# Copying a partial sum out of its PSUM bank, spreading GpSimd's weighings over three experts, and moving one addition ahead of a transposition

## The chip, the cores and the metric

The kernel runs on one core of a Trainium2 chip. The metric is the device time of one execution in microseconds; lower is better. Three timed runs of the kernel before gave 933.78, 928.51 and 932.78, so the median is 932.78 us. The execution that the profiler recorded took 928.73 us, of which 927.0 lie between its first and its last instruction.

## The reference

Two blocks follow each other. The first is an attention with polynomial sketches: 4 batches, 4 heads, 1088 positions, head dimension 32. Its output, laid out as 4352 tokens of 128 numbers, is the `x` of the second block, a mixture of experts that is balanced by Sinkhorn iterations:

```
logits = x @ w_gate                      # 4352 tokens, 8 experts
P = exp(logits - logits.max())
for _ in range(8):                       # rows, then columns, are normalised
    P /= P.sum(1, keepdims=True) + 1e-09
    P /= P.sum(0, keepdims=True) + 1e-09
    P *= N / E
for e in range(E):
    h = np.maximum(x @ w1[e], 0.0)       # 128 -> 1024
    ye = h @ w2[e]                       # 1024 -> 128
    out += P[:, e:e + 1] * ye
```

All is fp32. Every token passes through all eight experts, so nearly all the work is the two layers of the experts.

## The kernel before

**Groups and experts.** The tokens stand along the free axis of `xT` (128 features by 4352 tokens). The list `groups` cuts the expert work into (first token, columns of a tile, tiles, experts, weighted). The first eight groups are plain: expert 0 for all tokens and expert 1 for the first 1280 tokens are computed before the weights P are known, and their unweighted results are kept in SBUF, in `kept[0]` and `kept[1]`. These eight run while attention and Sinkhorn still go on; a hand-written generator (`steps`, fed by `fill`) deals out the expert work a step at a time between the parts of attention and routing. Then follow five weighted groups of three tiles of 256 tokens (first tokens 1280, 512, 2048, 2816, 3584) with experts 1 to 7 (2 to 7 for the group at 512), and a last one of two tiles of 256 tokens at token 0 with experts 2 to 7. For a weighted group GpSimd multiplies the group's columns of `xT` with the row of P (`weigh`, line 693, tile `xe`), since a positive factor passes through the relu. One expert of a three-tile group takes about 18.7 us.

**A step.** In each step TensorE does one first-layer product into one of four banks named `a` (line 929), ScalarE applies the relu and writes it to SBUF (line 933, tiles `hb` and `hx`), and TensorE does second-layer products of eight steps before (line 1114) into four banks named `s`. The second layer is multiplied with fewer products by Strassen-like schemes: seven products for two tiles (function `seven`), twenty for three. VectorE forms the sums of relu blocks that such schemes need (lines 946 and 993), GpSimd the sums of the second layer's weights (tiles `ws`, lines 203 to 206 and 242).

**Ends of plain groups.** In a plain group of two tiles that uses the seven products (five groups: three with 416 columns, two with 384), bank 0 ends up with P1 in its lower 64 partitions, and P1 and others go together into the two output tiles `y1` and `y2`, which are columns of `kept`. The function `part_of_seven(g, k)` is called when bank k has got its last product. ScalarE copies what has to change partitions or be read twice; VectorE adds. `add_now` queues an addition for the current step, `add` for a later step at leisure. For k = 0 ScalarE makes `z` from the two halves of the bank (lines 762 and 763), and VectorE adds the bank to it (line 756, `z<-s,z`). For k = 1 ScalarE copies bank 1 to `m` (line 768), and VectorE adds P1, still in bank 0, and `m` into the lower half of `y1` (line 756, `kept<-s,m`). The pool of the banks holds one buffer for each name, so the next group's first product into bank 0 waits for the last reader of bank 0.

**Weighing what was kept.** Once P is known, the kept results must be weighted too. `weigh_kept(g)` does this for a weighted group: for each expert that the group doesn't compute itself (one, or two for the groups at tokens 512 and 0), it loads the row of P, broadcast to 128 partitions, through SyncE's queue (tile `pb`, line 689) and lets GpSimd multiply (line 693, `kept<-kept,pb`); then GpSimd adds two kept results to one (line 717), and for the last group forms a difference (line 720). All of it is called at one place in `steps`: in the first step of the group's fourth expert (third in the last group). GpSimd's instructions are kept in program order.

**The end.** `last_part(g, k)` assembles the last group. Bank 3 comes first, then 0, 2, 1. For k = 2 VectorE does two additions into `y2`, then `put(y2)` transposes it in blocks of 32 and stores it by four DMAs (two on SyncE's queue, two on ScalarE's), then VectorE adds to the upper half of `x`. For k = 1 it adds bank 1 and `x` into `y1`, transposes and stores it. In this last stretch, from the second last block on, VectorE, TensorE and ScalarE run in the order in which the program writes them; for VectorE and TensorE that also holds while attention and routing run.

Of the kernel before, what the change touches and what calls it, by code (L numbers as in the profile page):

```python
# [50 lines left out]
def kernel(  # L51
# [12 lines left out]
    nc = tc.nc  # L64
# [50 lines left out]
    own = consts.tile([P, H], F32, name="own")  # L115
# [36 lines left out]
    for i in range(2):  # L152
        t = wk.tile([P, H + 1, NT + 1, D], F32, name=f"v{i}", bufs=1)
# [487 lines left out]
    lower, upper = slice(0, H2), slice(H2, P)  # L641
# [17 lines left out]
    kept = [keep.tile([P, N], F32, name="kept0"), keep.tile([P, 1280], F32, name="kept1")]  # L659
# [4 lines left out]
    def direct_of(j):  # L664
        return items[j][0] in DIRECT
# [21 lines left out]
    def weights_of(e, lo, n, tag):  # L687
        pb = pools[0].tile([P, 3 * NT3], F32, tag=tag, name=tag)[:, 0:n]
        tc.keep_in_program_order(nc.sync.dma_start(out=pb, in_=pT[e:e + 1, lo:lo + n].to_broadcast([P, n])))
        return pb  # L690

    def weigh(out, x, pb):
        tc.keep_in_program_order(nc.gpsimd.tensor_tensor(out, x, pb, op=Alu.mult))  # L693
# [12 lines left out]

    first_weighted = next(j for j, (g, e) in enumerate(items) if g == PLAIN)

    def weigh_kept(g):

        lo, n, t, es, _ = groups[g]
        ys = []
        for e in range(es[0]):
            ys.append(kept[e][:, lo:lo + n * t])
            weigh(ys[e], ys[e], weights_of(e, lo, n * t, "pb"))
        for y in ys[1:]:
            tc.keep_in_program_order(nc.gpsimd.tensor_tensor(ys[0], ys[0], y, op=Alu.add))
        if t == 2:
            k1, k2 = ys[0][upper, 0:n], ys[0][upper, n:2 * n]
            tc.keep_in_program_order(nc.gpsimd.tensor_tensor(k1, k1, k2, op=Alu.subtract))  # L720

    def at_leisure(do):

        soon.append(lambda: later.append(do))

    def put(y, lo, n, queues):
        b0, nb = lo // 32, n // 32
        yt = pools[0].tile([P, NT3 // 32, 32], F32, tag="yt", name="yt", bufs=4)[:, 0:nb, :]
        nc.vector.transpose(out=yt.rearrange("p b d -> p (b d)"), in_=y)
        store(yt, b0, b0 + nb, queues)  # L730
# [13 lines left out]
    def room(tag, n=NMAX):  # L744
        return keep.tile([P, NMAX], F32, tag=tag, name=tag)[:, 0:n]

    def part_of_seven(g, k):

        lo, n, _, es, _ = groups[g]
        s = sums[g][k]  # L750

        def add(out, a, b):
            at_leisure(lambda: nc.vector.tensor_tensor(out, a, b, op=Alu.add))

        def add_now(out, a, b):
            soon.append(lambda: nc.vector.tensor_tensor(out, a, b, op=Alu.add))  # L756

        own = parts.setdefault(g, {})
        y1, y2 = (kept[es[0]][:, lo + t * n:lo + (t + 1) * n] for t in range(2))
        if k == 0:  # L760
            z = own["z"] = room("z", n)
            nc.scalar.copy(z[lower], s[upper])
            nc.scalar.copy(z[upper], s[lower])
            add_now(z, s, z)
            own["p1"] = s
        elif k == 1:
            m = own["m"] = room("m", n)
            nc.scalar.copy(m, s)
            add_now(y1[lower], own["p1"][lower], m[lower])
        elif k == 2:  # L770
            w, f = own["w"], own["f"] = room("w", n), room("f", n)
            nc.scalar.copy(w[lower], s[lower])
            nc.scalar.copy(f[lower], s[upper])
            nc.scalar.copy(f[upper], s[upper])
        else:
            r = room("r", n)
            nc.scalar.copy(r[upper], s[lower])
            own["r"] = r
            own["p7"] = s
        own[k] = True  # L780
        z, w, f, m = (own.get(x) for x in "zwfm")
        if all(own.get(x) for x in (0, 2, 3)) and "v" not in own:
            own["v"] = True
            add_now(w[upper], own["p7"][upper], own["r"][upper])
            add(z, z, w)
            add(y2, z, f)
        if all(own.get(x) for x in range(4)):
            add(y1[upper], z[upper], m[upper])
# [9 lines left out]
    def last_part(g, k):  # L798


        lo, n, *_ = groups[g]
        s0, s1, s2, s3 = sums[g]

        def add(out, a, b):
            nc.vector.tensor_tensor(out, a, b, op=Alu.add)

        (y1, y2), z, w, x, f, r = last_rooms(g)
        if k == 3:
            nc.scalar.copy(r[upper], s3[lower])
            add(w[upper], s3[upper], r[upper])  # L810
        elif k == 0:
            nc.scalar.copy(z[upper], s0[lower])
            nc.scalar.copy(f, s0)
            add(x[upper], z[upper], w[upper])
            add(z[upper], x[upper], s0[upper])
        elif k == 2:
            nc.scalar.copy(r[lower], s2[upper])
            nc.scalar.copy(x[lower], s0[lower])
            add(y2[upper], z[upper], s2[upper])
            add(y2[lower], s2[lower], r[lower])  # L820
            put(y2, lo + n, n, (nc.sync, nc.scalar))
            add(x[upper], x[upper], s2[upper])
        else:
            add(y1, s1, x)
            put(y1, lo, n, (nc.sync, nc.scalar))
# [295 lines left out]
    def second(k, p):  # L1121
        into(items[blocks[k][0]][0], *p)

    def steps():

        todo, sums_at, t = {}, {}, 0
        for k in range(len(blocks) + 5):
            if k == len(blocks) - 2:
                ctx.enter_context(tc.manual_schedule(engines={engines.DVE, engines.PE, engines.Activation}))
            if k == len(blocks):  # L1130
                for i, ps in enumerate(last_products()):
                    todo.setdefault(t + i, []).extend(ps)
            if k < len(blocks):
                j, q = blocks[k]
                g, e = items[j]
                lo, n, tiles, es, weighted = groups[g]
                if q == 0:
                    for i in (j, j + 1, j + 2 if 0 < j and j + 2 < first_weighted else j):
                        if i < len(items) and i not in sources and (pools or i < first_weighted):
                            prepare_x(i)  # L1140
                        if i < len(items) and i not in loaded_w and (pools or i < first_weighted):
                            prepare_w(i)
                if j == 0 and q == 2:
                    prepare_w(2)
                if q == 1 and j + 1 < first_weighted and not direct_of(j + 1) and loaded_w[j + 1][2] is None:
                    w1, w2, _ = loaded_w[j + 1]
                    w = w1, w2, sums_of_two(items[j + 1][1], w2)
                    loaded_w.update({i: w for i in loaded_w if items[i][1] == items[j + 1][1]})
                if q == 0:
                    if weighted and e == es[3 if tiles == 3 else 2]:  # L1150
                        weigh_kept(g)
                if k == len(blocks) - HELD:
                    kept_to_sums(g)
                m, step, sums_ = (four if tiles == 3 else two)(k)
                products = twenty if tiles == 3 else eight if g in DIRECT else seven
            for c in range(m if k < len(blocks) else 4):
                if k < len(blocks):
                    step(c)
                for do in sums_at.pop(t, ()):
                    do()  # L1160
                while soon:
                    soon.pop(0)()
                for b, p in todo.pop(t, ()):
                    second(b, p)
                if k < len(blocks) and c == 0:
                    for i in range(2, 10):
                        sums_at.setdefault(t + i, []).append(lambda i=i, f=sums_: f(i))
                    if k < len(blocks) - 2:
                        for i, ps in enumerate(products(k)):
                            todo.setdefault(t + LAG + i, []).extend((k, p) for p in ps)  # L1170
                share = n / 480 * (16 / 15 if g in DIRECT else 1)
                if k >= len(blocks):
                    while later:
                        later.pop(0)()
                elif later and (tiles == 3 or c % 2 or share > 0.9):
                    later.pop(0)()
                yield share
                t += 1
        while soon:
            soon.pop(0)()  # L1180
        while later:
            later.pop(0)()
# [105 lines left out]
```

## Time and profile before

| What | Value |
|---|---|
| time, median of three | 932.78 us |
| span of the profiled execution | 927.0 us |
| VectorE busy from 110 to 215 us | 90.09 of 105 us |
| ScalarE busy from 110 to 215 us | 57.18 of 105 us |
| GpSimd busy over the span | 211.3 us (23%) |
| last instruction of VectorE that computes | ends at 923.48 us |

The profile's engines are PE (TensorE's matmuls), PEld (its weight loads), DVE (VectorE), ACT (ScalarE), POOL (GpSimd) and SP (SyncE, which issues most DMAs). A row of a timeline gives the start in us from the first instruction, the duration, the engine, the source line, the operation, what is written and read by the program's names, the shape, how many instructions were merged into the row, and in brackets how long the engine stood idle before it and what released it. TensorE executes each fp32 matmul of the program as two records, and two halves of 64 columns run side by side, so that a row "x4" is one step of one layer.

By stages, attention lies mostly in the first 110 us, the five ends of plain groups lie at about 118, 141, 163, 182 and 203 us, Sinkhorn's iterations run beside them on VectorE until about 175 us, and weighted groups fill the time from 203 us to the end.

### The profile page before, as it was taken

What the parts mean: (1) busy time and instruction counts of PE and PEld (TensorE: products, weight loads), DVE (VectorE), ACT (ScalarE), POOL (GpSimd) and SP (SyncE); (2) the same over time, 40 slices, a digit from 0 to 9 for tenths busy, and PEclk for the clock granted to TensorE, in tenths of its full rate; (3) what the DMA queues carried; (4) which work ended last, traced back from release to release, by engine and by line L of the source; (5) the groups of instructions that cost most, each with busy time, mean ns of one, the idle gap of its engine ahead of it and who ended that gap; (6) DMA issues with size and microseconds to landing.
All of it is one profiled execution on the core that took longest, in us unless ns stands there. A gap on an engine that the chain in (4) does not pass through costs nothing.

```text
span 927.0 us, 18876 instructions
## 1 busy us (share of the span) xinstructions
PE 914.0 (99%) x7466; PEld 552.6 (60%) x7466; DVE 673.4 (73%) x1140; ACT 412.6 (45%) x888; POOL 211.3 (23%) x220
## 2 busy tenths in 40 slices
PE   9999999999999999999999999999999999999997
PEld 6777444456666666655555555555555555556886
DVE  7544688797879697685876666965657977768665
ACT  3333455554444454434544444544445444445443
POOL 3031300093546402030120101101010224320220
PEclk9999999999999999999999999999999999999999
DMA  9994100213354434453444434363434365553640
GB/s 252 310 273 153 52 1 1 76 56 109 125 166 159 154 130 144 133 186 110 148 126 155 147 121 136 114 189 125 148 109 155 101 200 183 172 181 92 173 153 12
DMA packets 91303, 128.13 MB, mean 138 GB/s; under 512 B 25392, under 2 KB 69504, under 8 KB 86480
## 3 DMA queue, kind: packets, MB, share of 16 engines
q1 hardware_dynamic: 88384, 121.42, 41.7%
q0 software_dynamic: 1600, 5.36, 2.0%
q8 instruction: 58, 0.95, 0.4%
q10 hardware_dynamic: 1232, 0.16, 0.1%
q14 instruction: 29, 0.24, 0.1%
HBM read 107.88 MB, written 19.05 MB: 137 GB/s over the span
## 4 chain that ended last, share of the span: by engine, by line
PE 95%; DVE 3%; ACT 1%; issue 1%; POOL 0%; DVEq 0%; ACTq 0%; POOLq 0%
PE a L929 49%; PE s L1114 42%; PE a L352 1%; PE a L477 1%; PE a L114 1%; DVE hb L993 1%; PE a L319 0%; DVE pqg L993 0%; PE s L384 0%; PE a L441 0%; ACT hb L933 0%; PE s L407 0%; DVE kept L756 0%; PE a L511 0%; PE a L390 0%
## 5 line engine op out<-in xcount | busy, mean ns | idle before, releaser
L929 PE MATMUL a<-xe,w 128*64 128x256 f32 (+1 forms) x2560 | 519.5, 470 | 0.0
L933 ACT ACTIVATE hb<-a 128x256 f32<-128x256 f32 (+4 forms) x408 | 195.3, 480 | 257.8 <-PE a L929 231.7
L933 ACT ACTIVATE hx<-a 128x256 f32<-128x256 f32 (+1 forms) x360 | 167.4, 465 | 214.2 <-PE a L929 193.8
L929 PEld LDWEIGHTS a<-xe,w 128*64 128x64 f32 x2560 | 208.2, 137 | 77.2 <-issue 1.4
L1114 PE MATMUL s<-hb,ws 128*64 128x256 f32 (+2 forms) x1248 | 214.1, 395 | 0.6 <-DVE hb L993 0.6
L993 DVE TENSOR_TENSOR hx<-hx 128x512 f32<-128x512 f32 (+1 forms) x204 | 157.6, 783 | 68.2 <-ACT hx L933 62.7
L1114 PE MATMUL s<-hx,ws 128*64 128x256 f32 x1280 | 206.0, 379 | 0.7 <-DVE kept L756 0.7
L993 DVE TENSOR_TENSOR hb<-hb 128x512 f32<-128x512 f32 (+1 forms) x204 | 134.5, 670 | 92.2 <-ACT hb L933 88.0
L693 POOL TENSOR_TENSOR xe<-xT,xe 128x768 f32<-128x768 f32 (+2 forms) x41 | 83.3, 2032 | 499.3 <-DMA xe<-pT 485.0
L1114 PEld LDWEIGHTS s<-hx,ws 128*64 128x64 f32 x1280 | 106.7, 137 | 97.4 <-issue 74.0
L1114 PEld LDWEIGHTS s<-hb,ws 128*64 128x64 f32 x1248 | 101.9, 137 | 103.4 <-issue 80.0
L1114 PE MATMUL s<-hb,w 128*64 128x256 f32 (+3 forms) x616 | 116.5, 406 | 2.7 <-DVE kept L756 2.7
L929 PE MATMUL a<-xT,w 128*64 128x416 f32 (+3 forms) x512 | 117.3, 462 | 0.1
L1114 PEld LDWEIGHTS s<-hb,w 128*64 128x64 f32 x616 | 54.0, 137 | 35.6 <-issue 15.2
L1114 PE MATMUL s<-hx,w 128*64 128x256 f32 x384 | 68.5, 379 | 0.0
L929 PEld LDWEIGHTS a<-xT,w 128*64 128x64 f32 x512 | 47.0, 137 | 28.4 <-issue 21.5
L242 POOL TENSOR_TENSOR ws<-w 128x256 f32<-128x256 f32 (+1 forms) x70 | 60.1, 894 | 14.7 <-DMA w<-in_moe_w_dram 10.6
L946 DVE TENSOR_TENSOR hb<-hb 128x416 f32<-128x416 f32 (+3 forms) x60 | 46.4, 774 | 18.7 <-ACT hb L933 10.4
L946 DVE TENSOR_TENSOR hx<-hx 128x256 f32<-128x256 f32 (+1 forms) x65 | 39.1, 607 | 24.4 <-ACT hx L933 23.2
L993 DVE TENSOR_TENSOR pqg<-hb 128x512 f32<-128x512 f32 x68 | 44.5, 696 | 0.0
L1114 PEld LDWEIGHTS s<-hx,w 128*64 128x64 f32 x384 | 34.4, 137 | 10.3
L993 DVE TENSOR_TENSOR pqg<-hx 128x512 f32<-128x512 f32 x68 | 37.4, 591 | 0.0
(183 smaller groups left out, 466.6 us busy)
## 6 DMA issues: line engine op xcount, KB each, us to landing
w<-in_moe_w_dram SPq DMA_DIRECT2D x82, 512.0 KB, 5.3
ws<-ws SPq DMA_DIRECT2D x34, 1024.0 KB, 5.0
xe<-pT SPq DMA_DIRECT2D x34, 384.0 KB, 4.1
ws<-ws SPq DMA_DIRECT2D x12, 512.0 KB, 4.7
ph<-qa SPq DMA_DIRECT2D x12, 288.0 KB, 5.4
rb<-qb SPq DMA_DIRECT2D x3, 1152.0 KB, 7.9
pb<-pT SPq DMA_DIRECT2D x6, 384.0 KB, 7.5
kx<-in_k_dram SPq DMA_DIRECT2D x4, 544.0 KB, 4.9
```

What stands on the lines that cost most here:

```text
L114: nc.tensor.matmul(warm[:, 0:P], ones, ones, start=True, stop=True)
L242: tc.keep_in_program_order(nc.gpsimd.tensor_tensor(ws[:, c:c + len(ns)], blocks(x), blocks(y), op=Alu.subtract if off else Alu.add))
L352: nc.tensor.matmul(pv[64 * s:64 * (s + 1), i], kp[0:n, H * t + h].rearrange("p i j -> p (i j)"), vx[0:n, slots[h], t, :], start=(t == 0 an ...
L477: nc.tensor.matmul(pn[64 * s:64 * (s + 1), t, 2 * i:2 * i + 2].rearrange("p h d -> p (h d)"), ph[:, i, s, 64 * t:64 * (t + 1)], kvs[b % 2] ...
L693: tc.keep_in_program_order(nc.gpsimd.tensor_tensor(out, x, pb, op=Alu.mult))
L929: nc.tensor.matmul(ph[sl], loaded_w[j][0][:, P * f + H2 * s:P * f + H2 * (s + 1)], sources[j][:, lo:hi], start=True, stop=True, tile_posit ...
L933: nc.scalar.activation(out=out, in_=ph, func=Act.Relu)
L946: nc.vector.tensor_tensor(out, a, b, op=Alu.subtract)
L993: nc.vector.tensor_tensor(out if not isinstance(out, tuple) else places(*out), places(*a), places(*b) if isinstance(b, tuple) else b, op=A ...
L1114: nc.tensor.matmul(sums[g][i][H2 * s:H2 * (s + 1), n * place:n * (place + 1)], w, x, start=c == 1, stop=c == per, tile_position=(0, H2 * s))
```

## The change

There are three edits.

1. In `part_of_seven`, for k = 0, ScalarE also copies the lower half of bank 0, which is P1, to a tile of SBUF (the room `x`, which the plain groups hadn't used), right behind the two copies for `z`. The addition for k = 1 then reads P1 from there. The bank is meant to be free once `z<-s,z` and the copy are done, without the wait for `m`.
2. `weigh_kept(g, i)` is called in three or two successive experts and does one piece each time: the first kept result in the group's second expert, the second (if there is one) in the third, and the sum (and difference) in the expert after that. GpSimd's long run in one place is to become shorter ones.
3. In `last_part`, the addition to the upper half of `x` stands ahead of `put(y2)`, so that `y1`, which needs `x`, doesn't follow it directly.

```diff
-    def weigh_kept(g):
+    def weigh_kept(g, i):
 
         lo, n, t, es, _ = groups[g]
-        ys = []
-        for e in range(es[0]):
-            ys.append(kept[e][:, lo:lo + n * t])
-            weigh(ys[e], ys[e], weights_of(e, lo, n * t, "pb"))
+        ys = [kept[e][:, lo:lo + n * t] for e in range(es[0])]
+        if i < len(ys):
+            weigh(ys[i], ys[i], weights_of(i, lo, n * t, "pb"))
+            return
         for y in ys[1:]:
             tc.keep_in_program_order(nc.gpsimd.tensor_tensor(ys[0], ys[0], y, op=Alu.add))
...
             nc.scalar.copy(z[lower], s[upper])
             nc.scalar.copy(z[upper], s[lower])
+            own["p1"] = room("x", n)
+            nc.scalar.copy(own["p1"][lower], s[lower])
             add_now(z, s, z)
-            own["p1"] = s
...
             add(y2[upper], z[upper], s2[upper])
             add(y2[lower], s2[lower], r[lower])
+            add(x[upper], x[upper], s2[upper])
             put(y2, lo + n, n, (nc.sync, nc.scalar))
-            add(x[upper], x[upper], s2[upper])
...
                 if q == 0:
-                    if weighted and e == es[3 if tiles == 3 else 2]:
-                        weigh_kept(g)
+                    if weighted and 1 <= es.index(e) <= es[0] + 1:
+                        weigh_kept(g, es.index(e) - 1)
```

## The prediction

> **What bounds the kernel now.** I read the page first (busy shares), then the busy time by stage, then what TensorE waited for, and last the timeline around each wait.
>
> ```profile
> PE 914.0 (99%) x7466; PEld 552.6 (60%) x7466; DVE 673.4 (73%) x1140; ACT 412.6 (45%) x888; POOL 211.3 (23%) x220
> PEclk9999999999999999999999999999999999999999
> ```
>
> TensorE is busy 99% at full clock, so only the moments when it stands still can be won without removing matmuls. The table by stage says where these are (time, then busy time and instructions of PE, PEld, DVE, ACT, POOL):
>
> ```profile
> 110.00:215.00 105.00, 101.55 (x648) 48.84 (x646) 90.09 (x149) 57.18 (x116) 22.69 (x23) 1.00 0.13 44
> 280.00:890.00 610.00, 609.45 (x4718) 358.51 (x4716) 449.36 (x767) 273.13 (x578) 127.39 (x89) 1.00 0.46 146
> ```
>
> From 110 to 215, where the plain groups end, PE lacks 3.45 us; in 610 us of weighted groups it lacks 0.55. TensorE's waits (total us, times, longest) name both:
>
> ```profile
> PE s L1114 <- DVE kept L756: 3.5, 4, 1.2
> PE s L1114 <- DVE hb L993: 0.6, 1, 0.6
> ```
>
> The first is P1's bank. One of the four waits in the timeline (start, us, engine, work):
>
> ```profile
> 139.68 0.92 PE L929 MATMUL a<-xT,w 128*64 128x416 f32 x4
> 140.17 0.58 DVE L756 TENSOR_TENSOR z<-s,z 128x416 f32<-128x416 f32 x1
> 140.67 0.57 DVE L756 TENSOR_TENSOR kept<-s,m 64x416 f32<-64x416 f32 x1
> 141.29 0.56 PE L1114 MATMUL s<-hb,w 128*64 128x416 f32 x1 [0.70 <-DVE kept L756]
> ```
>
> The next group's first second-layer matmul overwrites bank 0 only after the y1 addition (kept<-s,m) has read P1 there. The second wait follows a run of GpSimd work:
>
> ```profile
> 400.28 4.12 POOL L693 TENSOR_TENSOR kept<-kept,pb 128x768 f32<-128x768 f32 x2 [12.25 <-DMA pb<-pT]
> 400.42 4.25 DVE L993 TENSOR_TENSOR pqg<-hb 128x512 f32<-128x512 f32 x2
> 404.47 1.88 POOL L717 TENSOR_TENSOR kept<-kept,kept 128x768 f32<-128x768 f32 x1
> 404.60 2.30 DVE L993 TENSOR_TENSOR hb<-hb,pqg 128x512 f32<-128x512 f32 x1
> 406.31 2.27 POOL L693 TENSOR_TENSOR xe<-xT,xe 128x768 f32<-128x768 f32 x1
> 406.83 3.09 DVE L993 TENSOR_TENSOR hb<-hb 128x512 f32<-128x512 f32 x2
> 409.18 0.65 PE L1114 MATMUL s<-hb,ws 128*64 128x256 f32 x4 [0.55 <-DVE hb L993]
> ```
>
> VectorE's five instructions fill 9.6 us here; by their groups' means (856, 786 and 766 ns, which hold such slow ones too) they would need 4.0. GpSimd runs through from 400.28 to 408.58.
>
> **What the Trainium skill says.** "PSUM — Partial Sum Buffer", section "PSUM bank collisions raise a hardware error": accesses of two engines are kept apart by bank, not by address; the trace agrees: PE starts 0.05 us after the addition ends (141.24). "SBUF — State Buffer", section "Who interferes with whom": a VectorE instruction with two SBUF inputs and a GpSimd one that reads SBUF exclude each other for the whole instruction; one with a single SBUF input is free. The trace agrees: the lines above, and at 202.68 kept<-s,m (one input in PSUM) took 0.54 us with GpSimd at work, while z<-z,w (both in SBUF) took 1.65 at 186.43. "VectorE: DVE Perf Modes", section "The TRN2 errata": an fp32 tensor_tensor takes (N+151)/0.96 ns, 591 for 416 columns; the trace has 585 for z<-z,w undisturbed, and 571 for kept<-s,m. So reading P1 from SBUF makes the addition no shorter.
>
> **Part 1, P1 copied out.** Added: five ScalarE copies of 64 partitions, at 0.50 us (its neighbours L762, L763: 503 and 497 ns), 2.5 us in all. Moved: bank 0 comes free after z<-s,z and the copy, instead of after kept<-s,m. VectorE's order stays the same. A listed wait understates the loss: a matmul of 416 columns is drawn 0.51 us long, but starts follow each other in 0.35, so 0.16 is to be added (256 and 512 columns: 0.38 or 0.59 against 0.21). Group by group:
> - at 117.84 PE waits 1.19 us. The z addition ended at 115.05; all goes: 1.19+0.16 = 1.35.
> - at 140.60 it waits 0.70, but z itself ends at 140.75; what goes is 140.75 to 141.24: 0.49.
> - at 162.39 it waits 0.84; z ends at 162.68, kept<-s,m at 163.17: 0.49.
> - the group at 180 has no wait (bank free at 181.62, taken at 182.86): 0.
> - at 202.64 it waits 0.72; z ended at 200.35: 0.72+0.38 = 1.10.
>
> Together 3.43 us. Does the new copy bring a wait of its own? Behind it in ScalarE's queue stand a relu (L933), the m, w and f copies and the next relus; PE waits for relus through the four "a" banks, and for m, w, f before banks 1 and 2. The tightest "a" bank is the one freed by the relu ending at 114.97 and taken at 116.92: 1.95 us, against 0.5 added. m ended at 115.36 and its bank is taken at 120.47, f at 117.95 and 121.87; 1.36 earlier and 0.5 later still leaves over 2 us. Bank 3 waits for the w addition (ends 120.53, taken at 123.39). ScalarE is idle 9 to 10 us of the 17 between two group ends, so the 0.5 is caught up. Cost on the path: 0, upper bound 2.5. VectorE is 86% busy here, and it must keep up: between the ends it idles 2.3, 1.9 and 2.1 us of 17, more than the 1.35, 0.49 and 0.49 by which PE draws ahead. The fifth addition will now have two SBUF inputs beside GpSimd (0.54 may become 1.2), but nobody on the path waits for it any more, and from 203 to 215 PE takes VectorE's results 2.2 us or more after they are ready.
>
> **Part 2, weighing spread.** No instruction is added; eight weighings, two sums and a difference change place, most by one or two experts (18.7 us each, by the spacing of the xe rows). In the group at token 512, 6.0 us of GpSimd work in a row plus an xe (2.27) becomes three pieces, weighing (1.9 to 2.3), weighing, sum, each next to an xe, so a run is about 4.3 us at most. Before the run at 400 VectorE's sums came 5.3 us before TensorE took them (order of the program laid over the trace); 8.3 us of lock used this up, 4.3 should not. So this wait goes: 0.55+0.38 = 0.93. Against it stands that from 278.22 GpSimd runs 13.8 us (2.31+2.27+9.23) and TensorE doesn't wait; but 9.2 of these are ten short sums, between which VectorE gets in. In the other groups the only weighing moves from the end of expert 4 to the end of expert 2, where the margin is 4 to 5 us again and a weighing costs VectorE at most 2: 0. There the tail of the preceding group (about 30 additions) has mostly drained; its tightest point, 0.05 us at 732, lies some 15 us earlier and is not touched. In the last group the sum and difference (1.33+0.80) now come after the xe of the next but one expert: load issued at 878.84, 4.1 to land, 1.6+1.33+0.80, done at 886.7; TensorE takes them at 891.6. Bound: 0 to 0.5.
>
> **Part 3, x ahead of the transposition.** Same VectorE instructions at the end. y1 started 0.13 after x ended (922.44 to 922.57), since it needs x; now a transposition (0.45) lies between: 0.1 won. y2's stores are issued 0.45 later, two per queue in 0.89, done at 923.36, just as y1's begin (923.4): no collision. 0.1, bounds -0.2 and 0.1.
>
> **Sum.** 3.43+0.93+0.1 = 4.5 us. From 215 on, PE has no other wait that could swallow an earlier start; xe and sums of the first weighted expert are ready at 188.7 and 198.4 and taken at 191.9 and 203.4; even if they came no earlier, the 2.3 won by then would not use up the 3.2 and 5.0. 932.78-4.5 = 928.3. The four known executions (928.51, 928.73, 932.78, 933.78) have their middle at 930.76, 2.0 under the given median, so a new median is likelier below 928.3 than above: I take a quarter of that, 927.8.
>
> **Rivals.**
> - A (0.64): as above, 927.8.
> - B (0.20), VectorE takes the place of the bank: with 86% busy the next addition or sum (hb L946, 0.57 us of margin at 193.07) comes too late after each end, and only half of part 1 and part 2 is kept: 1.7+0.4, 930.7. For it: VectorE idles 0.3 us from 184 to 198. Against: the idle times above.
> - C (0.08), slower: bank 0 waits for something else as long as before, and the five copies go on the path, 2.5 us: 935.3. For it: ScalarE works without a break from 113.4 to 119.5. Against: the 1.95 us.
> - D (0.08), more is won: VectorE, freed of locks, also drops hidden delays: 7 us, 925.8.
>
> **Chances.** The bound for faster is 928.1. A gives faster three times in four with the scatter of 928.5 to 933.8 seen before (0.48, same 0.16); B faster 0.03, same 0.17; C slower 0.07, same 0.01; D faster 0.08. Sum: 0.59, 0.34, 0.07. The range reaches from 923.8 (928.5 less 4.7) to 931.5, past B; C and half of D's lower end stay out.
>
> **What would show it.** PE from 110 to 215 idle under 1 us, "s <- DVE kept L756" gone from its waits and at most two short ones for z left; no wait near 405; five new copies near 0.5 us; DVE busy much the same, POOL's longest run in the group at 512 near 4.3 us. Wrong: a new wait of PE for ACT or for DVE w or hb in 110 to 215, or for POOL kept near 888.

## The result and the profile after

| | before | after |
|---|---|---|
| median, beside the prediction's runs | 929.75 us (928.51 to 933.78) | 925.5 us (925.1 to 926.63), ratio 0.9948, interval 0.9926 to 0.997 |
| median, second comparison | 929.07 us (926.98 to 931.72) | 925.83 us (923.99 to 928.75), ratio 0.9965, interval 0.9954 to 0.9976 |

By the medians the change takes 4.25 and 3.2 us off. The ratio and its interval are estimated from all the runs of both kernels; in the first row, with six runs each, the quotient of the two medians alone would be 0.9954. The six runs of the kernel before in that row include the first three, with their median of 932.78; the three new ones (929.04, 930.37, 929.13) lie lower. Most of the spread between executions lies ahead of the edits, as shown below.

The profile page of the kernel after, in the same lines as those that the prediction shows of the kernel before:

```profile
PE 912.8 (99%) x7466; PEld 636.7 (69%) x7466; DVE 667.3 (72%) x1140; ACT 413.4 (45%) x893; POOL 211.3 (23%) x220
PEclk9999999999999999999999999999999999999999
```

ScalarE has five more instructions (893 instead of 888); all other counts are the same. Line numbers shift with each edit: L929, L993 and L1114 of the kernel before are L930, L994 and L1115 here. The table by stage of the kernel after (from and to, then sum, PE, PEld, DVE, ACT, POOL, clock, DMA share, GB/s):

```profile
110.00:215.00 105.00, 104.45 (x676) 54.69 (x674) 90.84 (x152) 59.48 (x124) 24.37 (x23) 1.00 0.13 43
280.00:890.00 610.00, 610.00 (x4728) 434.22 (x4726) 443.57 (x767) 273.12 (x579) 121.73 (x87) 1.00 0.47 145
```

TensorE lacked 3.45 us from 110 to 215 and now lacks 0.55; in the weighted groups it lacked 0.55 and lacks nothing. Of its waits for VectorE in these stages one line is left (total, times, longest):

```profile
PE s L1115 <- DVE z L756: 0.6, 2, 0.4
```

The same place in the timeline as the one shown in the prediction, the end near 141:

```profile
139.80 0.93 PE L930 MATMUL a<-xT,w 128*64 128x416 f32 x4
140.29 0.58 DVE L756 TENSOR_TENSOR z<-s,z 128x416 f32<-128x416 f32 x1
140.79 0.57 DVE L756 TENSOR_TENSOR kept<-x,m 64x416 f32<-64x416 f32 x1
140.93 0.56 PE L1115 MATMUL s<-hb,w 128*64 128x416 f32 x1 [0.20 <-DVE z L756]
```

The product no longer waits for the y1 addition, which reads `x` now; it starts 0.06 us after the z addition ends (140.87). Two more lines, near 116.5 and 202, show the other effects of the copy on VectorE:

```profile
116.55 0.59 DVE L756 TENSOR_TENSOR z<-s,z 128x416 f32<-128x416 f32 x1 [0.60 <-ACT x L765]
...
201.80 1.08 DVE L756 TENSOR_TENSOR kept<-x,m 64x384 f32<-64x384 f32 x1
```

The z addition now waits for the new copy too, though it needs nothing of it. The copy reads bank 0 as well and stands ahead of the addition in the program; no run takes apart which of the two makes it wait. The prediction hadn't seen this. It had seen that the y1 addition could become longer beside GpSimd: near 202, with GpSimd at work, it took 1.08 us (0.54 before, from PSUM). TensorE waits for neither at these two places.

GpSimd in the group at token 512, after:

```profile
360.62 1.86 POOL L693 TENSOR_TENSOR kept<-kept,pb 128x768 f32<-128x768 f32 x1 [9.84 <-DMA pb<-pT]
365.76 2.34 POOL L693 TENSOR_TENSOR xe<-xT,xe 128x768 f32<-128x768 f32 x1 [3.27 <-DMA xe<-pT]
378.42 1.82 POOL L693 TENSOR_TENSOR kept<-kept,pb 128x768 f32<-128x768 f32 x1 [10.32 <-DMA pb<-pT]
384.38 2.08 POOL L693 TENSOR_TENSOR xe<-xT,xe 128x768 f32<-128x768 f32 x1 [4.14 <-DMA xe<-pT]
386.42 2.00 POOL L717 TENSOR_TENSOR kept<-kept,kept 128x768 f32<-128x768 f32 x1
```

The longest run is 4.0 us (384.38 to 388.42), and the run of 8.3 us is gone.

**A common measure.** The span is a poor measure for 1 us: the matmul with which the comparison below begins, ahead of the first edit's place, started anywhere from 106.9 to 110.5 us in the fourteen traces of this study, by waits in attention that no edit touches. So each trace is cut at the same matmuls, and the times between their starts are compared (us, worked out from the starts in the traces). In the first trace of the kernel before, the cuts of the first four rows lie at 107.21, 121.87, 143.47, 165.21 and 203.82. The last column is the least value in any of the fourteen traces; what a stretch takes beyond it is called its loss below.

| from one matmul to another | before, four traces | after, two traces | least of all |
|---|---|---|---|
| end at 118 | 14.66 | 13.19, 13.20 | 13.19 |
| end at 141 | 21.59 to 21.60 | 21.11, 21.10 | 20.67 |
| end at 162 | 21.74 to 21.75 | 21.25, 21.26 | 20.58 |
| ends at 180 and 203 | 38.58 to 38.61 | 37.64, 37.64 | 37.64 |
| around 409 | 214.03, 213.43, 213.79, 214.03 | 213.22, 213.22 | 213.22 |
| around 732 | 26.47, 26.28, 26.28, 26.28 | 26.47, 26.28 | 26.28 |
| around 883 | 21.58, 22.07, 22.28, 21.90 | 21.58, 21.58 | 21.58 |
| first matmul to the end of the span | 819.75, 819.38, 819.97, 819.80 | 815.50, 815.31 | |

The four traces of the kernel before are its first one, the two repeats, and the kernel with part 3 alone, which differs only at the very end. By this measure the change is worth 819.72 less 815.41, 4.3 us: 3.4 in the first four rows, the rest at 409 and 883. The row at 732 comes and goes in both kernels and isn't the change's. The times of the first four rows add up to the same within 0.05 us in all traces of one kernel; the part at 409 and 883 differs from trace to trace. Why the second pair of medians shows only 3.2 us stays open; a few traces can't tell how the stretch ahead of the first cut is spread over many executions.

### The profile page after: what moved, and what is told of

It reads as the page before. It is cut to its first block, busy times and chain, and to the rows that moved or that the text cites. A ratio compares the mean times of both kernels' runs of the same rounds, so it can differ in the third digit from the quotient of the medians.

```text
span 924.3 us, 18883 instructions
## 1 busy us (share of the span) xinstructions
PE 912.8 (99%) x7466; PEld 636.7 (69%) x7466; DVE 667.3 (72%) x1140; ACT 413.4 (45%) x893; POOL 211.3 (23%) x220
## 4 chain that ended last, share of the span: by engine, by line
PE 93%; DMA 3%; DVE 2%; SPq 0%; issue 0%; ACT 0%; ACTq 0%; DVEq 0%
PE a L930 49%; PE s L1115 42%; DMA qx<-in_q_dram 1%; DMA kx<-in_k_dram 1%; DMA qb<-qab 1%; DMA v<-in_v_dram 1%; PE a L477 1%; PE a L352 0%; DVE qT L302 0%; PE a L511 0%; PE a L319 0%; PE a L441 0%; DVE hb L947 0%; ACT hb L934 0%; DVE cs L617 0%
## 5 line engine op out<-in xcount | busy, mean ns | idle before, releaser
L930 PE MATMUL a<-xe,w 128*64 128x256 f32 (+1 forms) x2560 | 537.3, 470 | 0.0
L930 PEld LDWEIGHTS a<-xe,w 128*64 128x64 f32 x2560 | 244.4, 137 | 40.3 <-issue 1.4
L1115 PE MATMUL s<-hb,ws 128*64 128x256 f32 (+2 forms) x1248 | 222.0, 395 | 0.0
L1115 PE MATMUL s<-hx,ws 128*64 128x256 f32 x1280 | 213.7, 379 | 0.0
L994 DVE TENSOR_TENSOR hx<-hx 128x512 f32<-128x512 f32 (+1 forms) x204 | 155.1, 771 | 69.1 <-ACT hx L934 63.6
L994 DVE TENSOR_TENSOR hb<-hb 128x512 f32<-128x512 f32 (+1 forms) x204 | 135.1, 673 | 94.4 <-ACT hb L934 90.3
L1115 PEld LDWEIGHTS s<-hx,ws 128*64 128x64 f32 x1280 | 124.8, 137 | 77.7 <-issue 64.8
L1115 PEld LDWEIGHTS s<-hb,ws 128*64 128x64 f32 x1248 | 120.0, 137 | 84.1 <-issue 70.4
L1115 PE MATMUL s<-hb,w 128*64 128x256 f32 (+3 forms) x616 | 118.7, 406 | 0.6 <-DVE z L756 0.6
L930 PE MATMUL a<-xT,w 128*64 128x416 f32 (+3 forms) x512 | 117.5, 462 | 0.2
L1115 PEld LDWEIGHTS s<-hb,w 128*64 128x64 f32 x616 | 58.7, 137 | 28.1 <-issue 14.5
L1115 PE MATMUL s<-hx,w 128*64 128x256 f32 x384 | 70.7, 379 | 0.0
L930 PEld LDWEIGHTS a<-xT,w 128*64 128x64 f32 x512 | 47.6, 137 | 27.5 <-issue 19.5
L994 DVE TENSOR_TENSOR pqg<-hb 128x512 f32<-128x512 f32 x68 | 43.7, 684 | 0.0
L1115 PEld LDWEIGHTS s<-hx,w 128*64 128x64 f32 x384 | 38.9, 137 | 5.7
L994 DVE TENSOR_TENSOR pqg<-hx 128x512 f32<-128x512 f32 x68 | 35.2, 558 | 0.0
```

Source lines behind the costliest of these rows:

```text
L930: nc.tensor.matmul(ph[sl], loaded_w[j][0][:, P * f + H2 * s:P * f + H2 * (s + 1)], sources[j][:, lo:hi], start=True, stop=True, tile_posit ...
L994: nc.vector.tensor_tensor(out if not isinstance(out, tuple) else places(*out), places(*a), places(*b) if isinstance(b, tuple) else b, op=A ...
L1115: nc.tensor.matmul(sums[g][i][H2 * s:H2 * (s + 1), n * place:n * (place + 1)], w, x, start=c == 1, stop=c == per, tile_position=(0, H2 * s))
```

## The experiments

### One part alone

**Copy alone**: the kernel before with

```diff
+            own["p1"] = room("x", n)
+            nc.scalar.copy(own["p1"][lower], s[lower])
             add_now(z, s, z)
-            own["p1"] = s
```

> The kernel before with part 1 alone (P1 copied out of bank 0 by ScalarE; weighing and end as before). Theory (the bank was what TensorE waited for, and the parts add up): TensorE's wait for kept is gone at all five group ends, two short waits for z of 0.2 to 0.4 us remain, TensorE is idle under 1 us from 110 to 215, and the time is 3.4 us below the kernel before, which is 0.8 us of the change's 4.25 short of it. The wait for hb near 405 to 409 stays, at about 0.5 us. Rival (VectorE takes the bank's place, and only together with the spread weighing does the copy bring its full gain): a wait for hb or w appears between 110 and 215, or the hb wait near 409 grows by about as much as TensorE comes earlier, and the gain is 2 us or less.

Measured: 925.82 us against 928.75 of the kernel before, ratio 0.9973 (0.9963 to 0.9983), so 2.9 us less and not 3.4. TensorE from 110 to 215 is that of the changed kernel:

```profile
110.00:215.00 105.00, 104.45 (x676) 54.90 (x674) 91.48 (x153) 59.39 (x124) 24.80 (x24) 1.00 0.14 48
280.00:890.00 610.00, 610.00 (x4730) 448.94 (x4727) 451.09 (x769) 273.14 (x579) 125.29 (x88) 1.00 0.47 145
```

The rival, VectorE in the bank's place, falls: no wait for hb or w appears. But the theory's second half falls too. The second line shows no idle TensorE from 280 to 890, although GpSimd's run of 8.4 us is still in one piece:

```profile
398.24 0.68 DVE L994 TENSOR_TENSOR hb<-hb,pqg 128x512 f32<-128x512 f32 x1
398.56 4.25 POOL L693 TENSOR_TENSOR kept<-kept,pb 128x768 f32<-128x768 f32 x2 [13.65 <-DMA pb<-pT]
398.84 4.53 DVE L994 TENSOR_TENSOR hb<-hb 128x512 f32<-128x512 f32 x2
```

In the first trace of the kernel before, the run began with VectorE still at the start of its chain of sums: the two for pqg and the hb<-hb,pqg fell into the run and took 6.6 us. Here the two for pqg were done when it began, and the third had started.

**Spreading alone**: the kernel before with the edits on `weigh_kept`:

```diff
-        for e in range(es[0]):
-            ys.append(kept[e][:, lo:lo + n * t])
-            weigh(ys[e], ys[e], weights_of(e, lo, n * t, "pb"))
+        ys = [kept[e][:, lo:lo + n * t] for e in range(es[0])]
+        if i < len(ys):
+            weigh(ys[i], ys[i], weights_of(i, lo, n * t, "pb"))
+            return
...
-                    if weighted and e == es[3 if tiles == 3 else 2]:
-                        weigh_kept(g)
+                    if weighted and 1 <= es.index(e) <= es[0] + 1:
+                        weigh_kept(g, es.index(e) - 1)
```

> The kernel before with part 2 alone (weighing of the kept results spread over three experts). Theory (length of GpSimd's run in the group at token 512): the four waits for kept stay at 3.5 us in all, the wait for hb at 409 is gone, GpSimd's longest run in that group is 4 to 4.5 us, and from 280 to 890 TensorE has no idle time over 0.05 us; the time is 0.8 to 0.9 us lower, less than such a comparison tells surely from none, so the waits decide. Rival (the wait at 409 went in the changed kernel because TensorE and VectorE stood differently to each other after part 1, not because of the spreading): the wait for hb near 409 is still there, at 0.3 us or more.

Measured: 928.53 against 928.75 us, ratio 0.9993 (0.9982 to 1.0004), which can't be told from no change. The trace shows four waits for kept of 3.4 us in all, none for hb, and no idle TensorE from 280 to 890:

```profile
280.00:890.00 610.00, 610.00 (x4725) 396.24 (x4723) 441.14 (x768) 273.74 (x579) 125.38 (x88) 1.00 0.47 147
```

From the first matmul to the end it is 818.84 us, 0.9 less than the mean of the traces of the kernel before. The copy alone is 4.3 below that mean (815.44, mean of two traces), and the whole change also 4.3: the parts taken singly add up to more than the whole. In both kernels the loss at 409 and 883 was gone or nearly so; the next section shows that with the copy alone this was the chance of a DMA's landing.

**Order alone**: the kernel before with

```diff
             add(y2[lower], s2[lower], r[lower])
+            add(x[upper], x[upper], s2[upper])
             put(y2, lo + n, n, (nc.sync, nc.scalar))
-            add(x[upper], x[upper], s2[upper])
```

> The kernel before with part 3 alone (the addition to x ahead of the transposition of y2). Theory: from the end of the lower y2 addition to the end of y1's transposition 0.1 us less than before (2.29 instead of 2.39), but from there to the end of the span only 0.04 less, since the stores of y2 are now issued later and y1's stand directly behind them in the two queues. Rival (the prediction's 0.1 reaches the end, and the changed kernel's 0.04 had another cause): from the addition's end to the span's end 0.1 us less. Everything ahead of the end is that of the kernel before; the group at token 512 gives a fourth pair of start and wait for hb.

The last instructions of this kernel:

```profile
921.99 0.42 DVE L805 TENSOR_TENSOR y<-s,r 64x256 f32<-64x256 f32 x1
922.43 0.42 DVE L805 TENSOR_TENSOR x<-x,s 64x256 f32<-64x256 f32 x1
922.89 0.45 DVE L729 STREAM_TRANSPOSE yt<-y 128x256 f32<-128x256 f32 x1
923.36 1.84 SPq L887 DMA_DIRECT2D out_dram<-yt  x4
923.37 0.42 DVE L805 TENSOR_TENSOR y<-s,x 128x256 f32<-128x256 f32 x1
...
923.83 0.45 DVE L729 STREAM_TRANSPOSE yt<-y 128x256 f32<-128x256 f32 x1
```

From the start of the lower y2 addition to the end of y1's transposition it is 2.29 us (before 2.39), to the end of the span 5.82 (before 5.87, after 5.83). SyncE's four issues, two of y2 and two of y1, now take 1.84 us in one row; before they took 2.31 with a pause. From the end of y1's transposition to the end of SyncE's last issue it is 0.93 us, where it was 0.84. So about half of the 0.1 is lost behind the transposition, as expected, where the issues of y1 now stand directly behind those of y2.

### Is the wait at 409 the run's length?

The kernel before, twice more, unchanged (928.01 and 932.28 us):

> The kernel before once more, unchanged, to see how steady its wait for hb at 409 is. In the first trace GpSimd's run of weighings in the group at token 512 began at 400.28, when VectorE still had three sums to form ahead of the one that TensorE took late; with the copy alone the same run began 1.4 us later in TensorE's own time (the row of P landed 9.0 instead of 7.5 us after its issue), the three sums were formed before it, and TensorE didn't wait. Theory (the wait is a coincidence with the landing of a DMA): in this execution the run starts elsewhere by some tenths to 1.5 us, and the wait is absent if it starts 1 us or more later, present if it starts at the same place. Rival (the run's length makes the wait, and the copy removed it in another way): the wait for hb near 409 is there at 0.5 us whatever the start. Waits from 110 to 215: the same four for kept, 3.4 to 3.5 us in all.

> The kernel before a third time, for the same question: a third pair of GpSimd's start in the group at token 512 and TensorE's wait for hb. Theory (coincidence with the landing): the wait follows the start, 0.5 us where the run starts as in the first trace, none where it starts 1 us or more later. Rival (length): 0.5 us each time.

The first repeat, the second trace of this kernel, in which the run began earlier:

```profile
398.76 4.03 POOL L693 TENSOR_TENSOR kept<-kept,pb 128x768 f32<-128x768 f32 x2 [11.13 <-DMA pb<-pT]
...
407.45 1.48 DVE L993 TENSOR_TENSOR hb<-hb 128x512 f32<-128x512 f32 x2
```

No wait for hb is listed: the run ended at 406.98, ahead of the last two sums, which took 1.48 us instead of 3.09. The stretch still lost 0.21 us. The third trace, in the last group:

```profile
881.95 2.95 POOL L693 TENSOR_TENSOR kept<-kept,pb 128x512 f32<-128x512 f32 x2 [7.72 <-DMA pb<-pT]
...
886.65 0.65 PE L1114 MATMUL s<-hx,w 128*64 128x256 f32 x4 [0.27 <-DVE hx L946]
```

This is a wait that the first trace didn't have at all. Now all kernels with the weighing in one piece are put together: the start of GpSimd's run after a fixed matmul (the one at 397.23 in the first trace, and for the last group the one at 877.74), and what the stretch lost against the least of all (us):

```
group at 512    start  1.75  1.93  2.89  3.05  3.26  4.48
                lost   0.05  0.21  0.81  0.81  0.57  0.01
                trace  copy2 2nd   order 1st   3rd   copy
last group      start  0.44   0.49  0.59  0.62  0.80  0.97  1.13  1.35
                lost   0      0     0     0     0.16  0.32  0.49  0.70
                trace  second 1st   fills copy  copy2 order 2nd   3rd
```

(1st to 3rd are the three traces of the kernel before; copy and copy2 the two of the copy alone; order is the kernel with the order alone; fills and second are the kernels of the next two sections.) In the last group each tenth of a microsecond of a later start beyond 0.64 costs a tenth. In the group at 512 the loss grows with a later start, until the run begins so late that VectorE's chain is through. The kernels with the copy lie on the same curves as those without it. So the first part did not remove the wait; where the landing of the rows of P put the run did. From the first load's issue to the run's start it was 7.6 us in the first trace, 9.0 and 6.2 in the two traces of the copy alone. The issue itself hadn't moved: in all the traces of the upper rows it stands 4.50 or 4.48 us ahead of the same matmul, with and without the copy. The theory of coincidence stands, except that an early start is nearly harmless as well, which it had not said. Length alone falls as the cause.

Length may still count: the last group has a sign of it. In the two traces in which a spread weighing began latest there (0.74 and 0.86 on the same scale, with three copies and with the whole bank), the stretch lost 0.04 and 0, where the line above gives 0.10 and 0.22 for a run in one piece. Two points are few.

### Reading or running?

> The kernel before, but in the group at token 512 GpSimd's two weighings and the sum of the kept results are replaced by nine fills of the pb tile with zeros (three for each), which write SBUF and read none of it; so the weighting of that group's kept results is left out. The fills wait for the same loads, so they begin at about 400 too. Theory (GpSimd's reading of SBUF holds VectorE's two-input sums off): VectorE's five instructions beside the run take about 4 us, as undisturbed, instead of 9.6, and there is no wait for hb near 409. Rival (GpSimd's writing, or its mere running, does it): the same five take 7 us or more, and the wait can be there.

```diff
-            weigh(ys[e], ys[e], weights_of(e, lo, n * t, "pb"))
+            pb = weights_of(e, lo, n * t, "pb")
+            if lo == 512:
+                for _ in range(WRITES):  # 3
+                    tc.keep_in_program_order(nc.gpsimd.memset(pb, 0.0))
+            else:
+                weigh(ys[e], ys[e], pb)
...                                      # the same for the sum of the two
```

```profile
401.46 4.61 POOL L719 MEMSET pb<- 128x768 f32 x6 [13.34 <-DMA pb<-pT]
402.05 1.48 DVE L1003 TENSOR_TENSOR hb<-hb 128x512 f32<-128x512 f32 x2
...
406.12 2.33 POOL L725 MEMSET pb<- 128x768 f32 x3
```

In this kernel the kept results of the group at 512 stay unweighted. The two sums at 402.05, beside the fills, took 1.48 us; the same two at 398.84 in the copy alone, beside the weighings at nearly the same phase, 4.53. So GpSimd's fills, which only write, don't hold VectorE's two-input sums off; its instructions that read do. That TensorE didn't wait proves nothing here: the fills began at 4.14 on the scale above, too late to meet the first three sums.

### The run at another place

```diff
-                    if weighted and e == es[3 if tiles == 3 else 2]:
+                    if weighted and e == es[1 if tiles == 3 else 2]:
```

> The kernel before, with the weighing of the three-tile groups still in one run but in the group's second expert instead of the fourth (last group as before). Theory (it is the run beside an xe that delays VectorE's sums, wherever it stands, and its start that decides by how much): in the group at 512 TensorE loses 0.2 to 0.8 us near 371 or nothing if the run starts 1.5 us later than VectorE's four-sum chain, and nothing at 409. Rival (something at 409 itself, the weights' transfers for instance, makes that wait): the loss at 409 stays at 0.5 to 0.8 us and none appears near 371.

```profile
364.99 4.26 POOL L693 TENSOR_TENSOR kept<-kept,pb 128x768 f32<-128x768 f32 x2 [9.66 <-DMA pb<-pT]
...
371.68 3.10 DVE L993 TENSOR_TENSOR hb<-hb 128x512 f32<-128x512 f32 x2
...
374.03 0.65 PE L1114 MATMUL s<-hb,ws 128*64 128x256 f32 x4 [0.56 <-DVE hb L993]
```

The wait moved with the run, and the stretch lost 0.82 us, as much as before at 409, where no wait is left. So this wait doesn't need anything that is special at 409. This is one execution, of 931.39 us.

### How much ScalarE can bear, and a freer bank

**Three copies**: the changed kernel with

```diff
-            nc.scalar.copy(own["p1"][lower], s[lower])
+            for _ in range(3):
+                nc.scalar.copy(own["p1"][lower], s[lower])
```

> The changed kernel with the copy of P1 made three times over, so that ScalarE has 1.0 us more to do at each of the five ends, 5 us in all, all of it ahead of the release of bank 0. Theory (the copy lies beside TensorE's work): at 118 and 203, where the bank was free 0.5 us or more ahead, TensorE still doesn't wait; at 141 and 162, where the z addition now waits for ScalarE, the two waits may grow by the part of the 1.0 us that lands in front of the addition; in sum TensorE loses at most 2 us of the 5, and none to relu outputs. Rival (ScalarE's work at the ends is on the path): TensorE waits for ACT at four or five ends, and loses 4 us or more.

From the first matmul to the end it was 818.28 us in the one execution, 2.9 more than the changed kernel: neither the theory's 2 at most nor the rival's 4 or more. All lay in the stretches of the ends at 141 (22.65 instead of 21.11, which begins at about 122) and at 203 (39.06 instead of 37.64); the ends at 118 and 162 lost nothing. Two waits of it:

```profile
122.38 0.59 DVE L756 TENSOR_TENSOR w<-s,r 64x416 f32<-64x416 f32 x1
...
123.03 0.56 PE L1116 MATMUL s<-hb,ws 128*64 128x416 f32 x1 [0.67 <-DVE w L756]
...
203.14 0.65 PE L1116 MATMUL s<-hx,ws 128*64 128x256 f32 x4 [0.36 <-DVE z L756]
```

So one copy of 0.50 us is free and two more of them are not: bank 3 waits for the w addition, and bank 0 at 203 for the z addition. The first of the two starts at the end near 118: VectorE stands idle there for 2.21 us ahead of the z addition (0.60 with one copy), which starts only after the third copy, and with its order kept it comes late to w. One copy alone had already used up much of that slack: in the changed kernel w ends at 122.56 and its bank is taken at 123.51, 0.95 us apart, where it was 2.86 before.

**Whole bank**: the changed kernel with

```diff
-            nc.scalar.copy(own["p1"][lower], s[lower])
-            add_now(z, s, z)
+            nc.scalar.copy(own["p1"], s)
+            add_now(z, own["p1"], z)
```

> The changed kernel, but ScalarE copies the whole of bank 0 (128 partitions) and the z addition reads this copy too, so the bank comes free after ScalarE's three copies alone. Theory (the two waits that are left, 0.20 and 0.35 us of idle TensorE at 140.7 and 162.0, are for the z addition, and no other wait stands close behind): both go, TensorE is idle under 0.15 us from 110 to 215, and the time is 0.6 us (with the 0.16 us of overlap that each wait adds, 0.87) below the changed kernel, 4.8 to 5.2 below the kernel before; the copy of 128 partitions takes the same 0.50 us as one of 64. Rival (VectorE is the next limit): a wait for hb or w takes their place, and the time is that of the changed kernel within 0.3.

```profile
110.00:215.00 105.00, 105.00 (x680) 65.38 (x678) 92.38 (x153) 59.59 (x124) 25.88 (x24) 1.00 0.14 49
```

TensorE doesn't stand still from 110 to 215. The copy of 128 partitions took 506 ns at 416 columns (the one of 64 took 499). The stretches at 141 and 162 came down to 20.67 and 20.59, 1.1 us together, a little more than the 0.87 expected. The time was 925.21, ratio 0.996 (0.9947 to 0.9974): less gain than the trace. In the last comparison the kernels stood side by side.

> The changed kernel once more, side by side with the copy alone and with the copy of the whole bank. From the first nine traces: between the fifth group end (203) and the last products TensorE lost 0.2 to 1.5 us in the kernel before (at 409 and, in three of four looks, at 883), and 0 at both in every kernel with the spread weighing. Theory (part 1 is worth 3.4, part 2 about 1.0 in the mean over executions, part 3 0.04): 4.4 us below the kernel before, no idle TensorE at 409 and 883, 13.19, 21.11, 21.25 and 37.64 us for the stretches around the five ends as in the first look. Rival (part 2 is worth nothing once part 1 is in, since the copy alone showed no loss at 409 or 883 either): 3.4 below, and the copy alone gives the same time within 0.3 us.

> The kernel before with part 1 alone, a second look. Theory (the losses at 409 and 883 come and go with the landing of the rows of P, so the copy alone has them in some executions): a loss of 0.2 to 0.8 us at 409 or at 883 in this look is likely, and the median lies 0.5 to 1 us above the changed kernel's. Rival (TensorE's and VectorE's new standing after part 1 removes them for good): no loss at either place again, and the median is the changed kernel's within 0.3 us.

> The changed kernel with the whole of bank 0 copied and the z addition reading the copy, side by side with the changed kernel. In its first trace TensorE had no idle time at all from 110 to 215, 1.1 us less than the changed kernel over the ends at 141 and 162. Theory: 1.0 us below the changed kernel here, 5.4 below the kernel before. Rival (its first median, 3.5 below the kernel before, says the gain is lost elsewhere): within 0.3 us of the changed kernel.

| | median | ratio to before | first matmul to the end |
|---|---|---|---|
| before | 929.07 us | | 819.72, mean of four traces |
| changed kernel | 925.83 us | 0.9965 (0.9954 to 0.9976) | 815.50, 815.31 |
| copy alone | 925.65 us | 0.9959 (0.9947 to 0.9972) | 815.34, 815.53 |
| whole bank | 923.38 us | 0.9938 (0.9926 to 0.9951) | 814.23, 814.19 |

Here the whole bank beats both kernels, by 2.4 us the changed one. The traces show 1.2 of it behind the first matmul, 1.1 at the ends of groups; the two profiled executions differ by a further 0.7 ahead of that matmul, where the edits don't reach, and whether the rest of the medians' difference lies there too isn't shown. The changed kernel's 3.2 us are nearer the 3.4 of its rival than the 4.4 of its theory. The copy alone, which had been expected 0.5 to 1 us above the changed kernel, equals it within 0.2 us, as its rival had said, with losses of 0.05 at 409 and 0.16 at 883 in its trace. So no median shows a gain of the spread weighing once the copy is in. What is left open is how often the kernel with the copy but the run in one piece meets a bad start; two traces (0.01 and 0.21 us lost) against four without the copy (0.7 to 1.3) are too few. If the start alone decides, as the curves and the unmoved issue say, all traces with the run in one piece may be taken together, and the mean loss is 0.41 us at 409 and 0.21 at 883: the spread weighing would be worth about 0.6 us, an estimate from these traces.

## Why the prediction was right

**What bounds the kernel: right for P1's bank, half right for the wait for hb.** Both waits went, but the second comes and goes without the change.

**Part 1: right, 3.4 us.** Forecast 1.35, 0.49, 0.49, 0 and 1.10 for the five ends; measured 1.46, 0.49, 0.49 and 0.94 for the last two together. The two that stayed waits for z were met exactly. The small misses are the term added for the overlap of matmuls: it was 0.16 at 118 and 0.38 at 203; measured loss less listed wait is 0.27 and 0.22 there, and 0.26 at 409, where 0.38 had been taken. That the new copy costs nothing was right, for the copy as made. The stated bound was no empty one: with two more copies, 2.9 of 5 us came onto the path, partly through bank 3 and the w addition, which the prediction named with a slack of about 2.9 us, without taking off that TensorE would come earlier and VectorE later (0.95 was left). It overlooked that the copy would also hold the z addition back.

**Part 2: near the forecast size in four traces, at partly another place and for an incomplete reason.** Forecast 0.93 at 409 and 0 in the last group. The four traces of the kernel before lost 0.81, 0.21, 0.57 and 0.81 at 409 and 0, 0.49, 0.70 and 0.32 at 883, in the mean 0.60 and 0.38; no trace with the spread weighing lost more than 0.04 at either. That the sum over the two places comes close to the 0.93 is in part luck: over all traces with the run in one piece it is about 0.6, and the medians show none of it beside the copy. The step that failed is "8.3 us of lock used this up": it made the run's length the cause, from one trace. The start within VectorE's chain decides (a run of 8.4 us lost 0.01), and it moves with a DMA's landing. The exclusion of GpSimd's reads and VectorE's two-input sums, taken from the Trainium skill's "SBUF — State Buffer", section "Who interferes with whom", is borne out, and so is what that section says of a GpSimd instruction that only writes (1.48 us for two sums beside fills, 4.53 beside weighings).

**Part 3: mis-sized, 0.04 instead of 0.1.** The transposition ended 0.1 earlier as forecast, but this didn't reach the end in full. The term that was left out is in the queues: y2's issues do end before y1's begin, as "no collision" had it, but y1's, right behind them, end later after the transposition (0.93 us instead of 0.84 on SyncE).

**The level.** 927.8 forecast, 925.5 measured, with a gain of 4.5 forecast and 4.25 measured. The starting value makes up the 2.3 and a little more: the kernel before came down by 3.0 to 929.75 with more runs, and only 0.5 of that had been allowed for; the gain, 0.25 smaller than forecast, goes the other way. The level is also luck in another sense: 925.5 lies next to the 925.8 of rival D, and only the gain and the trace tell the two apart. And its 928.1 for "faster", half a per cent below 932.78, was met by the level alone; half a per cent below 929.75 is 925.1, which 925.5 just misses.

**The rivals.** B (VectorE in the bank's place) falls by the copy alone. C (copies on the path) falls for one copy, and begins to come true at three (2.9 us). D isn't seen: VectorE dropped no hidden delay from 110 to 215 beyond the forecast waits.

## What to carry to other kernels

When a buffer is held by an instruction that itself waits for something else, the one value that it needs can be copied out by an engine with slack; here that took 0.50 us and freed the buffer. Then see which reader is last (here z), since copying all that is read went 1.1 us further at the same price. A wait of half a microsecond seen in one trace may depend on where a transfer happened to land: take a second and a third trace before giving it to a part of a change, and cut the traces at the same instructions, since spans differ by more than that. Test an engine's slack by adding the work again: the second and third copy were not free.

## What the runs showed of the hardware

- The same broadcast load of 384 KB, issued at the same place of TensorE's work (4.50 or 4.48 us ahead of one matmul), had its reader start between 6.2 and 9.0 us after its issue.
- GpSimd filled 128x768 fp32 in 0.74 us and multiplied two such tiles element by element in 1.8 us undisturbed. Two sums of VectorE with both inputs in SBUF took 1.48 us beside the fills and 4.53 beside the multiplications.
- A ScalarE copy out of PSUM took the same for 64 and 128 partitions (499 and 506 ns at 416 columns).
